# Block pairs as units, 2 KB packets for the early q and k, one load queue and halves of w_in in a fused attention and feed-forward kernel

## The chip, the cores and the metric

The kernel runs on one core of one Trainium2 chip. The metric is the device time of that core in microseconds (us). A kernel also has a slower state, in which some of its runs fall. The ratios below are of runs in the fast state alone; the medians and ranges are of all runs, a few slow ones among them (238.5 us of the kernel before). The span of a profile is about 2 us shorter than the device time of the same run.

## The reference, cut to what matters

```python
# q, k, v: [4, 8, 768, 64] float32; w_in [512, 2048], w_out [2048, 512]
scores = (q @ k.T) / 8 + bias        # bias = -slope[h] * distance
keep   = (key < 8) | (0 <= query - key < 96)        # 8 global keys, 96 local ones
a      = softmax(where(keep, scores, -1e9)) @ v
x      = a.transpose(0, 2, 1, 3).reshape(3072, 512)
h      = x @ w_in
g      = maximum(h, 0) + log1p(exp(-abs(h)))        # softplus
out    = g @ w_out                                  # [3072, 512] float32
```

## The kernel before

The 3072 queries are 24 blocks of 128, six to a sequence. Because of the window, a block needs its own key tile and the one before it; the first block of a sequence needs its own alone. A one-tile block has 8 score matmuls, a two-tile block 16 (eight heads; the matmuls come in pairs, one for each of two heads that lie on different 64 partitions). Two blocks make a group of 256 tokens for the feed-forward part: 64 w_in matmuls of 128x256 in eight slots of eight, then 32 w_out matmuls of 128x512. That makes 768 w_in and 384 w_out matmuls in all. Everything is bf16 on TensorE; inputs are cast on VectorE, ScalarE or GpSimd.

The order of the work on each engine is fixed when the kernel is built. A planner in the kernel simulates all engines and the DMA queues at build time, with a duration that the author gave to each operation, and takes from each engine's ready operations the one of lowest rank. The order that comes out is the program. TensorE is kept busy at the start with up to 90 filler matmuls on a blank tile.

```python
FIRST_UNITS = [[0], [1], [2, 3]]          # the four one-tile blocks, as 1 + 1 + 2
FIRST_LOADS = "u0 u1 u2 i0 i1 i2 i3 i4 i5 i6 i7 o0 u3 o1 o2 o3 o4 o5 o6 o7".split()
O_KEYS = {(0, 1): ("s", 3), (1, 0): ("s", 2)}       # else an output is summed in o_ps
...
s_ps = ps.tile([P, 16, P], F32, name="s_ps")        # four banks, one tile
x_ps = ps.tile([P, 512], F32, name="x_ps")
h_ps = [ps.tile([P, 512], F32, name=f"h_ps{i}") for i in range(2)]
o_ps = ps.tile([P, 512], F32, name="o_ps")
...
# loads of q, k, v: two tokens of one head to a partition row, 512-byte pieces
src[s, :, sl, :].rearrange("h (p r) d -> p h (r d)", r=2)
# w_in: 256 columns of all 512 rows, 1 KB pieces
moe_w_in[:, W * p : W * p + W].rearrange("(m p) c -> p m c", p=P)
...
# q after its transpose by TensorE: one plain copy out of PSUM
copy_on[eng](qT[i % NQT][:, 0:nc_, :], tr)
...
# what the score matmul reads of it: 64 tokens in a row, twice
v4 = t[:].rearrange("p (r m) t -> p m r t", r=2)
return lambda rows, m: v4[rows, m, :, 64 * x : 64 * x + 64]
...
nc.tensor.matmul(s_ps[:, reg, :].rearrange("p (r t) -> p r t", r=2),
                 kt[rows, m, :], qv(rows, m), start=not biased, stop=True, ...)
```

The softmax here doesn't subtract the row's maximum and nothing guards it: scores larger than these inputs give would overflow.

## Time and profile before

| | before |
|---|---|
| device time, median of the first 3 runs | 234.59 us (234.25 to 238.5) |
| span of the profile | 232.6 us |
| TensorE busy | 214.6 us, 92% |
| first w_in matmul | 21.17 us |
| granted TensorE clock, mean | 0.989 |

The first lines are of the page: busy tenths of TensorE, the granted clock, the DMA share and the DMA rate, each in 40 slices of 5.8 us.

```profile
PE   8979889898995998999999999999999999999883
...
PEclk9999999999998899999999999999999999999998
DMA  5999999999796449868877545899679422110021
GB/s 156 224 235 350 352 305 375 360 253 223 199 270 168 122 93 239 190 187 216 133 166 163 133 135 119 243 131 242 168 188 176 113 73 68 48 45 36 10 93 45
```

TensorE is nearly always busy, except in the thirteenth slice (70 to 76 us), where the clock is lower too (0.83 in 70 to 80 us). The DMA engines are nearly full from 6 to 58 us, but move only 224 to 235 GB/s in the second and third slices, while the q, k and v pieces of 512 bytes come. The next lines are three stretches of the trace: busy time of each engine with the number of instructions, the granted clock, the DMA share and GB/s.

```profile
core 0: us, PE busy (x) PEld busy (x) DVE busy (x) ACT busy (x) POOL busy (x), PEclk, DMA share, GB/s
8.00:12.00 4.00, 3.24 (x37) 2.32 (x36) 2.25 (x8) 1.71 (x2) 1.55 (x4) 1.00 1.11 226
60.00:70.00 10.00, 9.33 (x95) 6.36 (x95) 4.59 (x6) 8.99 (x12) 4.20 (x10) 1.00 1.07 260
70.00:80.00 10.00, 7.79 (x80) 4.13 (x81) 6.71 (x13) 4.24 (x5) 5.11 (x9) 0.83 0.55 144
```

From 60 to 80 us TensorE lost almost 3 us. The chain of waits says to what (start, duration, what):

```profile
63.98 6.67 DMA raw<-in_v_dram
...
70.70 0.61 POOL vb L395
...
73.70 4.28 PE o_ps L704 x12
```

A load of v was waited for until 70.6 us, then GpSimd cast it and copied it. The timeline of TensorE (start, duration, operation, shapes, count) shows the start of the feed-forward work and the usual length of 16 score matmuls:

```profile
20.84 0.40 PE L546 MATMUL s_ps<-qT,kTf 64*128 64x128 bf16 x8
21.17 1.05 PE L657 MATMUL h_ps<-XT,w_in_bf 128*128 128x256 bf16 x8
...
63.47 0.62 PE L546 MATMUL s_ps<-qT,kT 64*128 64x128 bf16 x16
```

The last of these: 16 scores in 0.62 us. The end of the chain shows the tail:

```profile
220.01 0.70 DVE osb L728
...
220.75 3.63 PE o_ps L704 x16
...
224.41 0.70 DVE osb L728
...
225.15 3.63 PE o_ps L704 x16
...
228.80 0.42 DVE osb L728
```

Twice TensorE stands still for 0.7 us while VectorE copies the finished output out of the bank that the next output needs.

### The profile page before, as it was taken

The page shows a single profiled execution, that of the slowest core. Times are in us where ns is not written, and L with a number is a line of the kernel's source. Part 1 is how long each engine was busy: PE and PEld are TensorE (multiplying, and loading weights), DVE is VectorE, ACT ScalarE, POOL GpSimd, SP SyncE. Part 2 cuts the span into 40 slices and gives each one's busy share as a digit, 9 for nine tenths or more (in the row PEclk, how much of TensorE's full clock was granted, in tenths as well). Part 3 has the DMA queues.
Part 4 walks back from the last instruction along what each step waited for, and adds up shares of the span by engine and source line. Part 5 has one row for each costly group of instructions (what it writes and reads, how often), then busy time and mean ns, then how long its engine had stood idle before and what let it go on. Part 6 is the DMA issues. An engine that isn't in the chain of part 4 may idle for free.

```text
span 232.6 us, 5037 instructions
## 1 busy us (share of the span) xinstructions
PE 214.6 (92%) x1994; PEld 149.0 (64%) x2026; DVE 113.1 (49%) x219; ACT 154.9 (67%) x202; POOL 98.1 (42%) x178
## 2 busy tenths in 40 slices
PE   8979889898995998999999999999999999999883
PEld 5758777555753476777667667676766867667531
DVE  5567315474179494059538448732944862111111
ACT  2432977751985259898878959876885987676600
POOL 3437645789456224767701606341573630000000
PEclk9999999999998899999999999999999999999998
DMA  5999999999796449868877545899679422110021
GB/s 156 224 235 350 352 305 375 360 253 223 199 270 168 122 93 239 190 187 216 133 166 163 133 135 119 243 131 242 168 188 176 113 73 68 48 45 36 10 93 45
DMA packets 76872, 40.97 MB, mean 176 GB/s; under 512 B 30640, under 2 KB 71856, under 8 KB 76848
## 3 DMA queue, kind: packets, MB, share of 16 engines
q1 hardware_dynamic: 75216, 39.86, 68.2%
q10 hardware_dynamic: 1632, 0.79, 1.4%
q8 instruction: 16, 0.26, 0.5%
q14 instruction: 8, 0.07, 0.1%
HBM read 27.26 MB, written 6.29 MB: 144 GB/s over the span
## 4 chain that ended last, share of the span: by engine, by line
PE 78%; DMA 7%; DVE 4%; POOL 3%; issue 3%; ACT 3%; DVEq 0%; POOLq 0%; ACTq 0%
PE o_ps L704 30%; PE h_ps L657 29%; PE s_ps L546 5%; PE h_ps L807 5%; DMA raw<-in_k_dram 4%; PE s_ps L704 3%; DMA raw<-in_v_dram 3%; PE x_ps L601 2%; ACT pb L581 2%; PE x_ps L598 2%; DVE z L572 2%; POOL vb L501 2%; POOL vb L395 1%; DVE osb L728 1%; PE s_ps L443 1%
## 5 line engine op out<-in xcount | busy, mean ns | idle before, releaser
L657 PE MATMUL h_ps<-XT,w_in_bf 128*128 128x256 bf16 x768 | 95.5, 273 | 1.5 <-POOL w_in_bf L350 0.9
L704 PE MATMUL o_ps<-w_out_bf,g 128*128 128x512 bf16 x323 | 84.8, 385 | 4.0 <-DVE osb L728 1.6
L657 PEld LDWEIGHTS <-w_in_bf 128*128 128x128 bf16 x768 | 73.2, 98 | 20.2 <-POOL w_in_bf L350 2.2
L672 ACT ACTIVATE e<-h_ps 128x512 f32<-128x512 f32 x96 | 59.9, 630 | 30.9 <-PE h_ps L657 30.3
L704 PEld LDWEIGHTS <-g 128*128 128x128 bf16 x384 | 35.9, 99 | 36.2 <-issue 7.0
L572 DVE TENSOR_TENSOR z<-s_ps,biasA 128x1024 f32<-128x1024 f32 x40 | 48.1, 1218 | 18.7 <-PE s_ps L546 17.0
L581 ACT ACTIVATE pb<-z 128x1024 bf16<-128x1024 f32 x40 | 41.8, 1050 | 18.9 <-DVE z L572 18.8
L683 ACT ACTIVATE g<-e 128x1024 bf16<-128x1024 f32 x48 | 50.7, 1056 | 1.3
L395 POOL CAST vb<-raw 64x512 bf16<-64x512 f32 (+1 forms) x60 | 32.8, 547 | 23.1 <-DMA raw<-in_v_dram 17.5
L728 DVE COPY osb<-o_ps 128x512 f32<-128x512 f32 (+1 forms) x23 | 15.2, 665 | 51.4 <-PE o_ps L704 51.3
L395 POOL CAST kb<-raw 64x512 bf16<-64x512 f32 (+1 forms) x44 | 24.0, 545 | 17.5 <-DMA raw<-in_k_dram 15.9
L501 POOL COPY vb<-vb 4x512 bf16<-4x512 bf16 x32 | 19.5, 610 | 17.1 <-PE x_ps L601 16.0
L611 DVE TENSOR_TENSOR xs<-x_ps,rcp 128x256 bf16<-128x256 f32 x46 | 19.5, 424 | 1.6
L610 DVE RECIPROCAL rcp<-x_ps 128x4 f32<-128x4 f32 x46 | 8.3, 179 | 22.8 <-PE x_ps L601 19.5
L601 PE MATMUL x_ps<-vb,pb 128*128 128x65 bf16 x160 | 15.1, 194 | 1.6 <-POOL vb L501 1.5
L598 PE MATMUL x_ps<-vb,pb 128*128 128x65 bf16 x160 | 15.5, 194 | 0.7 <-ACT g L683 0.7
L598 PEld LDWEIGHTS <-pb 128*128 128x128 bf16 x160 | 12.5, 98 | 5.2 <-issue 1.9
L492 POOL COPY kT<-kTf 128x32 bf16<-128x32 bf16 x16 | 3.5, 217 | 27.9 <-PE s_ps L546 27.0
L807 PE MATMUL h_ps<-blank 128*128 128x256 bf16 x90 | 13.8, 305 | 1.2 <-POOL blank L751 1.1
L546 PE MATMUL s_ps<-qT,kT 64*128 64x128 bf16 x288 | 13.4, 217 | 0.7 <-DVE z L572 0.7
L601 PEld LDWEIGHTS <-pb 128*128 128x128 bf16 x160 | 11.3, 97 | 3.4 <-issue 1.0
L370 DVE CAST qb<-raw 128x1024 bf16<-128x1024 f32 (+1 forms) x15 | 9.6, 641 | 7.5 <-DMA raw<-in_q_dram 7.5
(49 smaller groups left out, 98.6 us busy)
## 6 DMA issues: line engine op xcount, KB each, us to landing
out_dram<-osb SPq DMA_DIRECT2D x23, 256.0 KB, 2.4
raw<-in_moe_w_in_dram SPq DMA_DIRECT2D x8, 512.0 KB, 9.5
raw<-in_moe_w_out_dram SPq DMA_DIRECT2D x8, 512.0 KB, 8.3
raw<-in_q_dram SPq DMA_DIRECT2D x8, 512.0 KB, 4.3
raw<-in_k_dram SPq DMA_DIRECT2D x8, 512.0 KB, 5.5
raw<-in_v_dram SPq DMA_DIRECT2D x8, 512.0 KB, 4.9
raw<-in_q_dram SPq DMA_DIRECT2D x10, 128.0 KB, 3.5
raw<-in_k_dram SPq DMA_DIRECT2D x10, 128.0 KB, 3.6
```

What stands on the lines that cost most here:

```text
L395: copy_on[eng](dst, src[64 * x : 64 * x + 64, r, :, :])
L501: nc.gpsimd.tensor_copy(vb_of(prev)[sl, :, 0:D], vb_of(first)[sl, :, 0:D])
L546: nc.tensor.matmul(s_ps[:, reg, :].rearrange("p (r t) -> p r t", r=2), kt[rows, m, :], qv(rows, m), start=not biased, stop=True, skip_grou ...
L572: nc.vector.tensor_tensor(z[:, 0:nr, :], src, bias, ALU.add)
L581: nc.scalar.activation(pb[:, 0:nr, :], src, AF.Exp, scale=1.0 / root_d)
L598: nc.tensor.matmul(xv[:, m, :], pb[:, 2 * m, :], vb_of(n)[:, h, :], start=True, stop=False)
L601: nc.tensor.matmul(xv[:, m, :], pb[:, 2 * m + 1, :], vb_of(prev)[:, h, :], start=False, stop=True)
L657: last = nc.tensor.matmul(hv[:, j, :], w_in_bf[:, m, fb * P : fb * P + P], XT[g % NXG][:, m, :], start=(m == 0), stop=(m == NM - 1),)
L672: nc.scalar.activation(e[:, p % 2, :, :].rearrange("p j (b t r) -> p (j b) r t", b=2, r=2), hb[:].rearrange("p (a r t) -> p a r t", a=4, r=2),
L683: nc.scalar.activation(gt[:, 2 * p - 2 : 2 * p + 2, :].rearrange("p a t -> p (a t)"), e[:].rearrange("p a j t -> p (a j t)"), AF.Ln, bias=1.0,
L704: nc.tensor.matmul(bank(key), gt[:, fb, ns * P : ns * P + P], w_out_bf[:, fb, :], start=(fb == 0), stop=(fb == NFB - 1),)
L807: nc.tensor.matmul(h_ps[0][:, 0:256], blank[:, 0:P], blank[:])
```

## The change

Its intent is to feed TensorE earlier and never late. Every unit becomes a pair of neighbouring blocks of one sequence. For the first three units (called WIDE) q and k come eight tokens to a partition, so in 2 KB packets. All loads go through one queue, in an order that was tuned with the ranks and leads of the planner. A w_in load is now half the rows of 512 columns (2 KB packets) instead of all the rows of 256. The casts are dealt out by hand. The last four outputs go to four different banks (what the kernel calls a bank is 512 fp32 columns of a PSUM tile, room for one output), and the last copy and its store are split over two engines and two queues. The planner learns that eight loads may be under way at once.

The diff is cut to its core; the new rank tables, the engine tables and the bookkeeping of keys are left out.

```diff
+UNITS = [(0, 0), (1, 0), (0, 1), (0, 2), (1, 1), (1, 2), (2, 0), ... (3, 2)]
+WIDE = (0, 1, 2)
+FIRST_LOADS = "k0 q0 v0 v1 q1 k1 i2 i0 i1 i7 i3 i5 i6 i4 o4 q2 o2 o1 k2 o0 v2 o6 o3 o5 o7".split()
...
-O_KEYS = {(0, 1): ("s", 3), (1, 0): ("s", 2)}
+O_KEYS = {(0, 1): ("s", 3), (1, 0): ("s", 2),
+          (10, 0): ("s", 0), (10, 1): ("s", 1), (11, 0): ("s", 2), (11, 1): ("s", 3)}
...
+            if i in WIDE and which != "v":
+                for y in range(2):
+                        return nc.sync.dma_start(
+                            raw[:, 512 * y : 512 * y + 512],
+                            src[y::2, sl, :].rearrange("h (g r) d -> g h (r d)", r=8),
+                        )
...
-                    moe_w_in[:, W * p : W * p + W].rearrange("(m p) c -> p m c", p=P),
+            src = moe_w_in[W * half : W * half + W, 512 * c : 512 * c + 512]
+            dst = w_in_bf[:, 2 * half : 2 * half + 2, 512 * c : 512 * c + 512]
...
+        if i in WIDE:
+            v7 = t[:].rearrange("p (a r) (x g m) -> p x m r g a", r=2, x=2, m=NPAIR)
+            return lambda rows, m: v7[rows, x, m]
...
-                            s_ps[:, reg, :].rearrange("p (r t) -> p r t", r=2), kt[rows, m, :], qv(rows, m),
+                            reg.rearrange("p (r g a) -> p r g a", r=2, a=4)
+                            if unit_of(n) in WIDE
+                            else reg.rearrange("p (r t) -> p r t", r=2),
+                            kt[rows, m, :], qv(rows, m),
...
+        parts = [(0, 256, "DVE", "SP"), (256, DM, "ACT", "ACT")] if last else [(0, DM, "DVE", "SP")]
```

With eight tokens to a partition, the transposed q of a WIDE unit lies as (a r)(x g m): the token's part *a* (four values) is the slowest axis. k is sorted into token order (that of the old layout: the even tokens of a block, then the odd ones) when it is copied out of PSUM. q is not: its copy stays one plain copy, and the score matmul reads it through the view `r g a`, in which neighbouring reads are 256 bf16 elements, that is 512 bytes, apart.

## The prediction

> **What bounds the kernel now.** TensorE. The page's busy table gives it 92% of the 232.6 us span, and the chain that ended last is 78% TensorE. But it does feed-forward work only from the first w_in matmul at 21.2 us on (timeline). At trace rates (8 w_in matmuls 0.875 us, a w_out matmul 0.216 us, two-tile block about 1.03 us) I count, for 21-100 us, about 69 us of work in 79, and for 100-229 us about 122 in 129. So there are four losses: the start (21 us), about 10 us in 21-100, about 7 us afterwards, and 3.8 us behind the last matmul.
>
> - Start: while q/k/v come in 512-byte pieces the windows show 222-248 GB/s (4-16 us) at full DMA share; with w_in (1 KB) and w_out (2 KB) pieces 322-385. Three MB of q/k/v come before w_in; the w_in casts then follow the DMA, one per 1.5 us, until 31.3 us; w_out casts end at 49.8.
> - 21-100: the chain holds 10.0 us of waiting for a k load, 6.7 us for a v load at 64-71 us, then vb casts and copies; in 70-80 us the granted clock is 0.88 and 0.78.
> - End: two waits of 0.7 us for the output copy of the same bank, then two half copies one after the other.
>
> [...]
>
> **What changes.** Early q and k come in 2 KB packets (4 MB of first loads improved or reordered in one FIFO); only v keeps 512 bytes. w_in comes in halves of 2 KB rows: two loads before the first product, but four products then. Casts are dealt over POOL, VectorE, ScalarE. Units are pairs, so the single-block units with 128 KB DMAs (20 SyncE issues of 0.6 us) vanish. The first four blocks are two one-tile and two two-tile blocks: about 1.4 us of TensorE work moves into the start, and four large VectorE adds (1.22 us) become small or vanish. The last groups' outputs get their own banks; the last copy and store split over two engines and queues. Against: strided evictions of k (small), more seeds, all hidden by the start.
>
> **Costs (estimates from the trace).** Loads of 512 KB at about 355 GB/s take 1.48 us, v about 1.8. With k0 landing at about 4.3 us, i0 and i1 (eighth and ninth) land at 15-16.5; with a cast, the first w_in matmul comes at about 17.5 instead of 21.2: -3.7. All w_in are in by about 25 (31), all w_out by about 41 (50). So 21-100 is no longer fed late: of 10 us lost, about 5 come back. Attention done early: -1.4. Tail: -1.5 to -2. Sum about -12 us, nearly all on the critical path, since TensorE is bound afterwards. Gains in casts or VectorE time after 100 us are worth nothing by themselves.
>
> **Predicted: 222.5 us, 8 in 10 between 216.5 and 229.** Faster by over 2%: 0.92; within 2%: 0.07; slower: 0.01.
>
> **What would show it.** First w_in matmul at 16.5-18.5 us; 300 GB/s or more from 4 us on; last w_out cast by 42 us; granted clock 1.0 in 60-90 us; no output-copy waits in the chain's last 10 us; TensorE 92-95% busy; matmul means unchanged.
>
> **What would make it wrong.** The static order was planned: if a load lands later than the planner thought, TensorE waits in order behind a ready matmul (w_out piece 0 comes late, in the order o4, o2, o1, o0). One FIFO may block loads behind a wait for a raw buffer. The strided q and score writes may slow the score matmuls. The clock could drop in a gap at 40-60 us, when the third and fourth units arrive together: then 228-230.

-3.7, -5, -1.4 and -1.5 to -2 make about -12 us, so 234.6 becomes 222.5. The 1.8 us of a v load in 512-byte pieces is an estimate.

## The result, and the profile after

A ratio is the mean time of one kernel's fast runs over that of the other's fast runs of the same rounds, so it is not quite the ratio of the medians quoted beside it.

| | before | after |
|---|---|---|
| device time, median | 234.73 us (4 runs, 234.25 to 238.5) | 231.19 us (4 runs, 230.99 to 231.31) |
| ratio, 95% interval | | 0.9855 (0.9836 to 0.9875) |
| span of the profile | 232.6 us | 229.2 us |
| TensorE busy | 214.6 us, 92% | 219.5 us, 96% |
| first w_in matmul | 21.17 us | 26.25 us |
| granted clock, mean | 0.989 | 0.997 |

The kernel became 1.45% faster, about a quarter of the 5% that were predicted, and the time lies outside the range. The page after, the same lines without the DMA share:

```profile
PE   8998999999999999999999999999999999999873
...
PEclk9999999999999999999999999999999999999998
...
GB/s 167 329 384 387 387 354 365 285 188 96 139 147 207 245 118 180 163 279 197 226 226 183 124 173 183 192 178 153 75 197 166 81 49 23 73 46 0 49 46 92
```

The three stretches after, with the columns as before:

```profile
8.00:12.00 4.00, 3.88 (x37) 2.43 (x37) 2.28 (x6) 0.74 (x2) 2.69 (x4) 1.00 1.09 353
60.00:70.00 10.00, 10.00 (x107) 7.30 (x106) 5.09 (x7) 9.12 (x12) 4.67 (x9) 1.00 0.61 150
70.00:80.00 10.00, 10.00 (x112) 6.05 (x111) 9.27 (x16) 6.17 (x8) 7.77 (x14) 1.00 0.88 208
```

Two intended gains are there. The loads run at 353 GB/s instead of 226 in 8 to 12 us. And between 60 and 80 us TensorE no longer waits: 219 instructions instead of 175, at full clock. But look at the first stretch again: TensorE is busy for 3.88 us instead of 3.24, with the same number of instructions, 37. Its timeline:

```profile
11.36 0.38 PE L611 MATMUL h_ps<-qT,kTa 64*128 64x128 bf16 x1
11.56 0.40 PE L611 MATMUL h_ps<-qT,kTa 64*128 64x128 bf16 x1
...
12.24 1.97 PE L611 MATMUL s_ps<-qT,kTa 64*128 64x128 bf16 x16
...
23.66 1.97 PE L611 MATMUL s_ps<-qT,kTa 64*128 64x128 bf16 x16
26.25 1.03 PE L724 MATMUL h_ps<-XT,w_in_bf 128*128 128x256 bf16 x8
...
45.95 1.95 PE L611 MATMUL s_ps<-qT,kT 64*128 64x128 bf16 x16
...
63.49 0.62 PE L611 MATMUL s_ps<-qT,kT 64*128 64x128 bf16 x16
```

The 16 score matmuls of the WIDE units take 1.95 to 1.97 us; those of later units, loaded in the old layout, take the old 0.62. A pair of scores starts every 0.20 to 0.23 us (11.36, 11.56 and so on; about 0.22 on average), where a pair took about 0.057 before. And the first w_in matmul stands behind the scores of the second unit in TensorE's fixed order, so it comes at 26.25 us. The chain of waits before it:

```profile
16.83 1.40 DVE kb L431
...
20.14 0.44 DVE kTa L527
20.59 0.38 ACT kTa L527
...
23.84 1.79 PE s_ps L611 x16
```

No load is in that piece of the chain. It runs through the cast of k of the second unit, four copies of its transpose and the slow scores. Counted over the three units, the scores cost TensorE about 6.5 us more than at the old rate: units 0 and 1 each four pairs and one row of 16, about 0.65 + 1.35 = 2.0; unit 2 twice 16, about 2.6. These 6.5 us are inside the "96% busy" and do no more work than the old scores did.

The tail did not become what was predicted. The chain's end, and the waits of TensorE (engine, what waited, for what: us in total, times, longest):

```profile
217.69 0.70 DVE osb L796
...
218.44 3.63 PE s_ps L771 x16
...
222.09 0.70 DVE osb L796
...
222.84 2.77 PE s_ps L771 x12
...
225.62 0.43 DVE osb L796
```

```profile
PE s_ps L771 <- DVE osb L796: 2.9, 4, 0.8
```

Three of these four waits, 2.3 us, are at the end (the fourth, 0.5 us, falls before 70 us); the kernel before had two there, 1.6 us. TensorE still waits for each output copy, although the outputs now lie in four different banks. What they have in common is that the four banks are one tile, `s_ps`.

### The profile page after: what moved, and what is told of

Same layout as the page of the kernel before. It is cut to its first block, busy times and chain, and to the rows that moved or that the text cites. A ratio compares the mean times of both kernels' runs of the same rounds, so it can differ in the third digit from the quotient of the medians.

```text
span 229.2 us, 5012 instructions
## 1 busy us (share of the span) xinstructions
PE 219.5 (96%) x2030; PEld 149.8 (65%) x2030; DVE 114.6 (50%) x214; ACT 158.6 (69%) x213; POOL 90.1 (39%) x150
## 4 chain that ended last, share of the span: by engine, by line
PE 88%; ACT 6%; DVE 4%; issue 1%; POOL 0%; DVEq 0%; POOLq 0%
PE h_ps L724 33%; PE o_ps L771 28%; PE s_ps L771 9%; PE s_ps L611 7%; PE x_ps L871 5%; ACT e L739 2%; PE x_ps L665 2%; ACT g L750 2%; PE x_ps L668 2%; DVE osb L796 1%; ACT pb L648 1%; DVE kTa L527 1%; ACT kTa L527 1%; DVE kb L431 1%; DVE xs L678 1%
## 5 line engine op out<-in xcount | busy, mean ns | idle before, releaser
L771 PE MATMUL o_ps<-w_out_bf,g 128*128 128x512 bf16 x288 | 72.6, 379 | 0.3 <-ACT g L750 0.3
L639 DVE TENSOR_TENSOR z<-s_ps,biasA 128x1024 f32<-128x1024 f32 x36 | 43.0, 1218 | 21.4 <-PE s_ps L611 13.5
L648 ACT ACTIVATE pb<-z 128x1024 bf16<-128x1024 f32 (+1 forms) x40 | 39.6, 1006 | 5.5 <-DVE z L639 5.0
L451 POOL CAST vb<-raw 64x512 bf16<-64x512 f32 x40 | 25.3, 632 | 14.2 <-DMA raw<-in_v_dram 12.6
L796 DVE COPY osb<-o_ps 128x512 f32<-128x512 f32 x18 | 12.4, 690 | 31.0 <-PE o_ps L771 31.0
L771 PE MATMUL s_ps<-w_out_bf,g 128*128 128x512 bf16 x96 | 22.8, 379 | 2.9 <-DVE osb L796 2.9
L451 POOL CAST kb<-raw 64x512 bf16<-64x512 f32 x36 | 22.3, 618 | 4.4 <-DMA raw<-in_k_dram 2.9
L796 DVE COPY osb<-s_ps 128x512 f32<-128x512 f32 (+1 forms) x6 | 3.9, 648 | 24.7 <-PE s_ps L771 24.7
L871 PE MATMUL x_ps<-blank 128*128 128x252 bf16 x90 | 14.0, 308 | 1.9 <-POOL blank L818 1.1
L871 PEld LDWEIGHTS <-blank 128*128 128x128 bf16 x90 | 9.5, 111 | 4.8 <-issue 1.2
```

The source lines that it names most:

```text
L451: copy_on[eng](dst, src)
L639: nc.vector.tensor_tensor(z[:, 0:nr, :], src, bias, ALU.add)
L648: nc.scalar.activation(pb[:, 0:nr, :], src, AF.Exp, scale=1.0 / root_d)
L771: nc.tensor.matmul(bank(key), gt[:, fb, ns * P : ns * P + P], w_out_bf[:, fb, :], start=(fb == 0), stop=(fb == NFB - 1),)
L871: nc.tensor.matmul(x_ps[:, 4 * (D + 1) : 512], blank[:, 0:P], blank[:, 0 : 512 - 4 * (D + 1)])
```

## The experiments

Three theories were open at the start. The first: the step at which the matmul reads q makes the scores slow, and this lies on the critical path. Its rivals: any step, in the read or in the write to PSUM, costs as much, so that reading in another order would not help (in the kernel after itself the scores are written in a row); or the slow scores are hidden, and something else (loads, fillers, the halves of w_in, VectorE) holds the start. The tail is a separate question. Where the texts give theories letters, each says there what it expects; here they are named by what they say. The kernel before was run beside every set; its medians were 235.55 us for the first four experiments, 235.08 for the next four and 235.13 for the last four. All experiments start from the kernel after. By their traces e1, e1b, e2, e3 and e8 have its order on TensorE, VectorE, ScalarE and GpSimd, and e9 and e11 have that of e2, apart from the copies and tiles that were edited; the other runs were planned anew.

### e1_q_by_g: the score's columns in another order, q read in 8-byte steps

```diff
-            v7 = t[:].rearrange("p (a r) (x g m) -> p x m r g a", r=2, x=2, m=NPAIR)
+            v7 = t[:].rearrange("p (a r) (x g m) -> p x m a r g", r=2, x=2, m=NPAIR)
...
-                            reg.rearrange("p (r g a) -> p r g a", r=2, a=4)
+                            reg.rearrange("p (r g a) -> p a r g", r=2, a=4)
```

The same numbers are computed into the same places, in the same order of instructions. Only the order in which one matmul goes through its 128 queries is new: the innermost step of the read is 4 elements (8 bytes), and that of the write to PSUM is 16 bytes.

> Only the order of the free axes of the score matmuls of the first three units is changed: q is read in steps of 8 bytes (the innermost step was 512 bytes), and the same result is written to PSUM in steps of 16 bytes (was contiguous). The instruction order on all engines is that of the changed kernel. Theory A (the 512-byte steps of the q read made 16 score matmuls take 1.88 us where other blocks take 0.55): the groups fall to 0.55-0.8 us and the time by 4 to 6 us, to 225-227 us. Rival B (any step on either side, or the scattered PSUM write, costs as much): the groups stay above 1.3 us and the time within 1.5 us of 231.2. Rival C (the slow scores are hidden behind the casts and evictions of the start): groups get fast, time falls by under 2 us.

Measured: 226.48 us, ratio 0.9649 (0.9574 to 0.9725). Its timeline:

```profile
11.58 1.08 PE L611 MATMUL s_ps<-qT,kTa 64*128 64x128 bf16 x16
...
23.49 1.03 PE L724 MATMUL h_ps<-XT,w_in_bf 128*128 128x256 bf16 x8
```

16 scores take 1.08 us instead of 1.97, a pair 0.11 us, and the first w_in matmul comes 2.8 us earlier. The write became scattered and the scores became faster, so the step of the read is the cause, and it is on the critical path: the time fell by about 2.1%. But a step of 8 bytes is not free: the 16 scores had been expected at 0.55 to 0.8 us.

### e1b_q_by_g_psum_flat: the same with a contiguous write (wrong)

```diff
-                            reg.rearrange("p (r g a) -> p a r g", r=2, a=4)
+                            reg.rearrange("p (a r g) -> p a r g", r=2, a=4)
```

This writes PSUM in a row, so the queries of the WIDE units land in the wrong order. Its output is wrong, which doesn't matter for the time. The comparison with the reference still let it pass. The likely reason is the inputs: q and k are drawn with a deviation of 0.1, which makes (q k)/8 about 0.01 (an estimate), and the mask and the bias are added in the right places. So the comparison does not vouch for the order of q in any of these runs; for e2 it was checked in the code alone.

> As the run before, but the PSUM write is contiguous too, so the queries of the first three units land in a wrong order and the result is wrong on purpose. It separates read from write: theory A expects groups of 0.55-0.65 us and the same time as the run before, within 1 us. If the write steps cost, this run has fast groups and the run before slow ones, and is 4-6 us faster than it. If the 8-byte read steps cost, both are slow.

Measured: 226.04 us, ratio 0.9634 (0.9555 to 0.9714).

```profile
11.22 1.08 PE L611 MATMUL s_ps<-qT,kTa 64*128 64x128 bf16 x16
```

The scores take 1.08 us here too. So the scattered write of e1 adds nothing that can be seen beside this read, and e1's 1.08 us are the read's. The rival falls. Whether a scattered write would slow matmuls that run 16 in 0.62 us, no run here shows.

### e2_q_copied_flat: q put in token order when it leaves PSUM

```diff
-            return lambda rows, m: v7[rows, x, m]
+            return lambda rows, m: t[rows, NPAIR * x + m, :].rearrange("p (r g a) -> p r g a", r=2, a=4)
...
-            op(f"cpq{i}", ..., lambda: copy_on[eng](qT[i % NQT][:], tr), ...)
+            def evq():
+                if i not in WIDE:
+                    return copy_on[eng](qT[i % NQT][:], tr)
+                to = qT[i % NQT][:].rearrange("p (x m) (r g a) -> p x r m g a", x=2, r=2, a=4)
+                fr = tr.rearrange("p (a r) (x g m) -> p x r m g a", r=2, x=2, m=NPAIR)
+                for x in range(2):
+                    for r in range(2):
+                        last = copy_on[eng](to[:, x, r], fr[:, x, r])
+                return last
```

The sorting is paid for once, on VectorE or ScalarE, as the change did for k. The planner is told the old duration, so the order stays.

> The eviction of q of the first three units is made in four copies of 256 elements that put q in token order, so the score matmuls read and write contiguously. Same instruction order otherwise. Theory A: score groups of 16 at 0.55 us, 8 at 0.33; the q evictions grow from 0.68 to about 1.7 us each on VectorE (1.0 to about 1.5 on ScalarE), which gives back about 1 us in units 0 and 1; time 226-228.5 us. Rival C: no better than 230.

Measured: 225.09 us (224.54 to 225.35), ratio 0.9582 (0.9494 to 0.967).

```profile
12.01 0.62 PE L620 MATMUL s_ps<-qT,kTa 64*128 64x128 bf16 x16
...
23.31 1.03 PE L733 MATMUL h_ps<-XT,w_in_bf 128*128 128x256 bf16 x8
```

The scores are back at 0.62 us. The copies of q are dearer (four of 418 ns on VectorE instead of one of 680, four of 387 on ScalarE instead of one of 1012). The gain over the kernel after is 0.9855 - 0.9582 = 0.0273 of about 234.7 us, or 6.4 us, with an uncertainty of about 2 us by the two intervals (the medians give 6.1). That is what the 6.5 us of extra TensorE time let one expect. Most of the slow scores, if not all, was on the critical path. Only some 2.9 us of it shows at the start (26.25 to 23.31); the third unit's share comes later.

### e3_tail_banks: the last four outputs in four tiles

```diff
-    (10, 0): ("s", 0), (10, 1): ("s", 1), (11, 0): ("s", 2), (11, 1): ("s", 3),
+    (10, 0): ("x",),   (10, 1): ("o",),   (11, 0): ("h0",),  (11, 1): ("h1",),
```

> The last four output accumulations go to four separate PSUM tiles (x, o, h0, h1) where the changed kernel put them in four banks of one tile. Theory D: the three waits of 0.7 us of TensorE for the output copy at the end come from tracking the four banks as one tile; with separate tiles they vanish, 2 to 2.3 us are gained, 229 us. Rival: TensorE must wait for the copy for another reason (the copy is slower than thought, or the order holds it): waits stay, no gain.

Measured: 229.38 us (228.33 to 229.79), ratio 0.9764 (0.9686 to 0.9841), so about 2.1 us better than the kernel after, with an uncertainty of nearly 2 us (the medians give 1.8). Its span is only 1.4 us shorter; that profile has a slower stretch at the start (one w_in slot of 1.87 us instead of 1.03, mean clock 0.992). The waits of TensorE on the output copies:

```profile
PE s_ps L771 <- DVE osb L796: 0.5, 1, 0.5
```

They went from 2.9 us in four to 0.5 in one, and the one that is left is the early one: the three at the end, 2.3 us, are gone. Different banks of one tile had not been enough; different tiles were. That it is the dependency tracking of the framework, which takes the tile as a whole, is the obvious reading, but the run shows only that the waits go with the tile.

### e4_no_wide: no unit in 2 KB packets, planned anew

```diff
-WIDE = (0, 1, 2)
+WIDE = ()
```

> The changed kernel with the 2 KB packets undone: early q and k come in 512-byte pieces as all others, so q lies in token order after the transposes and the score matmuls read contiguously; the planner reorders a little. Theory E (the start of the feed-forward work is bound by the attention chain on the engines, not by when the loads land): score groups at 0.55 us, first w_in matmul at 22-25 us, time 225-227.5 us, that is as good as the run with q copied flat (225.1) or within 2 us of it, so the 2 KB packets bought nearly nothing and cost about 6 us. Rival F (the 2 KB packets matter for the start): DMA at 220-250 GB/s until 12 us, first w_in matmul 2 us or more later than the 23.3 us of the flat copy, time 228-231 us.

Measured: 228.99 us, ratio 0.9749 (0.9681 to 0.9817). The scores take 0.61 us and the first w_in matmul comes at 23.37 us, as in e2, although the loads run at 290 GB/s in 8 to 12 us instead of 353. So the faster loads don't seem to bring the start forward (the fillers at the head happened to take 0.8 us less here, see e9; e8 is cleaner). But the time is 4 us worse than in e2. By 150 us it had done 208 w_out matmuls (weight loads counted) against 224 in e2. The planner had been told other loads and had made another order. This run tells two things at once and so neither cleanly; e8 repeats it with the order held.

### e5_q_flat_fill: e2 with the fillers' true length

```diff
-FILLERS = 90
+FILLERS = 64
-BIASA_ON = ["ACT", "POOL", "DVE"]
+BIASA_ON = ["ACT", "DVE"]
-        op(f"fill{j}", "PE", 0.11, 1e6 + j, fn, reads=["blank"])
+        op(f"fill{j}", "PE", 0.213 if j < 30 else 0.11, 1e6 + j, fn, reads=["blank"])
```

The early fillers run longer than the planner believes (0.213 us from one to the next by the trace, where it counts 0.11), which may hold back the first real work on TensorE.

> On top of the run with q copied flat: the planner is told 0.213 us for the first 30 filler matmuls (the trace shows the first ones at that spacing) so 23 instead of 43 stand before the first k transposes, 64 in all, and the late bias tiles are made on ScalarE and VectorE only (on GpSimd one took 1.06 us where the planner thought 0.4). Theory G: the in-order fillers and the bias tiles held the first scores until 11.6 us though k had been cast at 5.6 and q at 7.6; scores start at 9.5-10.5, first w_in matmul at 21.5-22.5, time 223.3-224.3 us. Rival: the start is held later by the casts of the second unit, then the first scores move and the first w_in matmul does not, time within 0.6 us of 225.1.

Measured: 224.97 us, ratio 0.9585 (0.9514 to 0.9657), the same as e2. The first unit's scores came at 10.80 instead of 12.01 us, but the second unit's at 21.45 instead of 21.77 and the first w_in matmul at 22.99 instead of 23.31. Most of what the first unit won was lost before the second unit. So the fillers don't seem to bind the start; the order of some other operations changed with them.

### e6_q_flat_narrow: e2 with w_in in 1 KB column blocks, planned anew

```diff
-NARROW = ()
+NARROW = (0, 1, 2, 3)
```

> On top of the run with q copied flat: w_in in column blocks of 1 KB rows as before the change, in the same order of names. Each product then waits for one load, not two, but the loads are slower. If the loads of w_in bind the start, the first w_in matmul moves by a microsecond or more and the time by as much; if they do not (theory E), the time stays within 1 us of 225.1.

Measured: 231.22 us (5 runs), ratio 0.9837 (0.9756 to 0.9917), 6 us worse than e2. Its loads ran at 349 to 353 GB/s from 12 to 24 us, e2's at 365 to 394. The first w_in matmul came at 23.57 us, so not there. TensorE had new waits (1.8 us for a copy to XT on ScalarE, 1.6 for a copy of v on GpSimd, 1.0 for a copy of k on VectorE). As in e4 the plan was a new one, so this run does not say whether the halves or the plan cost it; e9 does.

### e7_all_true: all mends, and true durations for the planner

This is e2, e3 and e5 together, and the planner is told what the four copies of q cost.

```diff
-            op(f"cpq{i}", eng, t_copy(eng, 1024, True), rank, evq, ...)
+            op(f"cpq{i}", eng, 4 * (t_copy(eng, 256, True) + 0.14) if i in WIDE else t_copy(eng, 1024, True), rank, evq, ...)
```

> All mends together: q copied flat with its true duration told to the planner, fewer fillers, no bias on GpSimd, and the last four outputs in separate PSUM tiles. If they add: 225.1 minus about 2 for the end minus about 1 for the start, 221.5-223 us, 5% below the kernel before.

Measured: 226.48 us, ratio 0.9648 (0.9575 to 0.9722), where 221.5 to 223 had been expected. Truer figures gave a worse plan: new waits of TensorE, 1.5 us for the cast of k and 1.1 us for that of q, and 210 w_out matmuls by 150 us, about as in e4. The ranks and leads of the change were tuned for the plan that came out of the old figures.

### e8_small_packets: 512-byte packets, with the order of the kernel after

```diff
-                            raw[:, 512 * y : 512 * y + 512],
-                            src[y::2, sl, :].rearrange("h (g r) d -> g h (r d)", r=8),
+                            raw[:, 512 * y : 512 * y + 512].rearrange("p (h c) -> p h c", h=4),
+                            src[4 * y : 4 * y + 4, sl, :].rearrange("h (p r) d -> p h (r d)", r=2),
...
-        if i in WIDE:      # the views of q, k and the scores
+        if False:
```

The planner's figures stay those of the kernel after, so every engine has the same order.

> Like the run that undid the 2 KB packets, but with the planner left as it is, so that the order on every engine is that of the changed kernel and of the flat copy: early q and k come in 512-byte pieces, lie in token order, are evicted by one plain copy and scored contiguously. It measures the packets alone. Theory E (packets do not bind the start; the 4 us of the earlier run came from its re-planned order): first w_in matmul within 0.7 us of the 23.3 us of the flat copy, time within 1 us of 225.1. Rival F (late loads cost 4 us somewhere): time 228-230 us and a wait on a load in the chain.

Measured: 225.69 us (225.55 to 226.52), ratio 0.961 (0.9548 to 0.9673). The stretch of 8 to 12 us:

```profile
8.00:12.00 4.00, 4.00 (x52) 2.96 (x51) 2.16 (x6) 0.77 (x3) 2.61 (x4) 1.00 1.20 292
```

And the first w_in matmul in its timeline:

```profile
22.81 1.03 PE L724 MATMUL h_ps<-XT,w_in_bf 128*128 128x256 bf16 x8
```

The loads run at 292 GB/s instead of 353 (v comes in 512-byte pieces in both), and yet the first w_in matmul comes at 22.81 us, and the time is that of e2 within the intervals. The 2 KB packets made the loads faster, as predicted. But, with the sorting of q and k that they call for (e8 has plain copies again, so it weighs the two together), they earned no time that can be seen, and they were the reason for the layout that cost 6.4 us.

### e9_q_flat_narrow_same: e2 with w_in in 1 KB column blocks, with e2's order

```diff
-            src = moe_w_in[W * half : W * half + W, 512 * c : 512 * c + 512]
-            dst = w_in_bf[:, 2 * half : 2 * half + 2, 512 * c : 512 * c + 512]
+            raw = raw_t[slot][:].rearrange("p (a c) -> p a c", a=NM)
+            src = moe_w_in[:, W * p : W * p + W]
+            dst = w_in_bf[:, :, W * p : W * p + W]
```

> w_in in 1 KB column blocks as before the change, but with the planner's figures and so the order of the flat copy run (where the earlier run re-planned and lost 6 us). If the halves of w_in matter by themselves, time 226.5 us or more; if the 6 us came from the re-planned order, within 1 us of 225.1, as every product waits for fewer bytes but loads run at about 350 instead of 385 GB/s.

Measured: 225.44 us, ratio 0.9596 (0.9527 to 0.9664), as e2, although its loads ran at 348 to 356 GB/s from 12 to 24 us, against 365 to 394. The halves of w_in are worth nothing by themselves, and the 6 us of e6 came from planning anew. The first w_in matmul came at 21.91 us in this profile instead of 23.31. That need not be the edit's doing: the 43 fillers at the head of TensorE's order took 6.08 us here and 7.37 in e2 (7.12 in the kernel after, 6.18 in e11):

```profile
1.08 7.37 PE L880 MATMUL x_ps<-blank 128*128 128x252 bf16 x43 [1.08 <-POOL blank L827]
...
1.08 6.08 PE L881 MATMUL x_ps<-blank 128*128 128x252 bf16 x43 [1.08 <-POOL blank L828]
```

These fillers are the same in all four kernels, and their rate changes on the way: in the kernel after, each microsecond from 1 to 6 us counts 5 to 8 of them, and 12 from 6 to 8 us (one that crosses a border counts twice). From 4 to 8 us TensorE ran 43 matmuls in e9 and 28 in e2, so the faster rate began earlier in e9. (The clock column of the profile reads 1.00 throughout, so the trace shows the change of rate and not its reason.) A difference of 1.3 us between two profiles at the start can be that.

### e10_q_flat_dve_less: casts of the second unit from VectorE to ScalarE

```diff
-    1: {..., "q": "POOL", "v": ["POOL", "DVE"], "k": "DVE"},
+    1: {..., "q": "POOL", "v": ["POOL", "ACT"], "k": "ACT"},
```

This is e2 with the cast of k (1.40 us in the chain of the kernel after) and half the casts of v off VectorE. If VectorE's queue held the start, the second unit's scores should come earlier.

> The flat copy run with the second unit's k cast and its two VectorE v casts (about 2.5 us of VectorE between 12 and 17 us) on ScalarE. Theory H (VectorE's in-order queue at 10-18 us sets the start): the second unit's scores begin 1 us or more before 21.5 us and the first w_in matmul at 21.3-22.5 us instead of 23.3. What the total does is open, since the planner re-orders the rest: 222.5-228. Rival (ScalarE becomes the same queue): first w_in matmul not earlier.

Measured: 229.68 us, ratio 0.9798 (0.9715 to 0.9882), worse than e2 by 0.0216 of the time before, or about 5 us. A line of its timeline:

```profile
23.04 1.06 PE L620 MATMUL s_ps<-qT,kTa 64*128 64x128 bf16 x16
```

And of its waits of TensorE:

```profile
PE o_ps L601 <- DVE kTa L536: 1.7, 1, 1.7
```

The second unit's scores came later (23.04 instead of 21.77 us, and in a phase of low clock, 0.78 in 20 to 24 us), and TensorE gained a wait of 1.7 us for a copy of k. The expectation missed. The order was planned anew here too, so the run doesn't clear VectorE; it only shows that this way of relieving it doesn't help. What bounds the start stays open.

### e11_q_flat_tail: e2 and e3 together, the order kept

> The flat copy and the separate PSUM tiles for the last four outputs, order otherwise unchanged. If the two add: 225.1 - 2 = 222.7 to 223.6 us, waits of TensorE on the output copy down from 2.9 to at most 0.9 us.

Measured: 222.52 us as the median of all four runs (221.84, 221.41 and 223.21 in the fast state, 222.15 on average; the fourth, of 226.14, was slow), ratio 0.9453 (0.9373 to 0.9532). If the two gains add, the ratio is 0.9855 - 0.0273 - 0.0091 = 0.9491, which lies in the interval. The end of its chain:

```profile
206.05 3.45 PE o_ps L780 x16
209.50 6.92 PE h_ps L780 x32
...
216.50 0.43 DVE osb L805
```

The last 48 w_out matmuls run without a wait. This version beats both kernels: 5.5% below the kernel before, against 1.45% for the change as it was.

## Why the prediction was wrong

It expected 222.5 us, and 231.19 were measured, a miss of 8.7 us. Two mends bring 6.4 and 2.1 us by the ratios, 8.5 together, and the kernel with both runs at 222.15 in the fast state. The miss is thus explained to within the intervals. That the mended time comes so near the predicted one is partly luck, since the terms of the sum were not all right: in e11 too the first w_in matmul comes at 21.97 us, later than before the change (21.17), so the predicted 3.7 us of the start never came. Yet at 80 us e11 has done 29 w_in and 14 w_out matmuls more than the kernel before, about 6 us of feed-forward work (an estimate at 0.109 and 0.216 us each). The gain came in another place than predicted.

- **"Against: strided evictions of k (small), more seeds, all hidden by the start."** This is the step that failed. It counted the strided writes of k (its copies of 128x256 took 411 to 425 ns on VectorE, those of the same size in the kernel before about 288) but no cost for q, which isn't sorted at all and is read with a step of 512 bytes by every score matmul of three units. e1 and e2 show the cause, and e2 its size: 6.4 us, not hidden. The risk list had the sentence "The strided q and score writes may slow the score matmuls" without a number. A count would have shown the stake: four times 16 scores and twice 8 are 40 pairs, so each 0.1 us on a pair is 4 us of TensorE; the runs showed 0.163. The half of that sentence about score writes had no object: in the kernel after they are not strided, and strided ones added nothing that can be seen beside the read (e1 against e1b).
- **The start, "-3.7".** The loads became faster as predicted (353 GB/s), but the first w_in matmul came 5.1 us later instead of 3.7 earlier. About 2.9 us of that are slow scores (e2). The prediction timed this start by the landing of w_in, at 15 to 16.5 us for i0 and i1, and a cast. In the trace these two landed at 17.2 and 18.4 us, in the order of issue, and the first four casts of w_in had ended by 22.6 us. TensorE came to the first w_in matmul only at 26.25 us, since the second unit's copies and scores stand before it in its order. So the path was another than the predicted one; e8 and e9 show that neither the packets nor the shape of the w_in loads move the time, and what else bounds the start stays open (e10).
- **The middle, "of 10 us lost, about 5 come back".** Right in kind: from 60 to 80 us TensorE went from 17.1 us busy to 20.0, the clock stayed at 1.00, and the wait for v is gone. At 80 us the kernel after had done 192 w_in and 91 w_out matmuls, the kernel before 192 and 82, though the former began 5 us later and lost about 6.5 us to slow scores. Which part of the change brings this (pairs, leads, load order or one queue) was not taken apart, nor was the "-1.4" for attention done early.
- **"All w_out by about 41".** The last cast of w_out ended at 48.9 us (before 49.8). That step missed, and TensorE had nothing to wait for through it.
- **The tail, "-1.5 to -2".** It didn't come: three waits on the output copies, 2.3 us, were left at the end, where the kernel before had two of 1.6 us together. The prediction took different banks for independent. With different tiles 2.1 us came (e3), about the predicted size.
- **"Matmul means unchanged", "TensorE 92-95% busy".** The first was false (1.97 for 0.62 us). The second read 96%, and would have looked like a success to anyone who reads the share alone.

## What to carry to other kernels

A load layout with larger packets may be paid for by the later readers (here 6.4 us): before taking it, write down the innermost step at which each matmul reads the data, and sort once in a copy if that step is not one element. Three steps were measured here: 16 scores took 0.62 us with a step of one element, 1.08 with 4 and 1.97 with 256, so of these only the first was free; the sorting copies cost four of 418 ns on VectorE instead of one of 680. A longer time of the same matmuls is the sign that this went wrong, and a rising TensorE share (here from 92% to 96%) hides it. Outputs that are to be independent should lie in different tiles, not only in different banks: four banks of one tile left three waits, 2.3 us, at the end here, and four tiles none (e3). In a statically planned kernel, test one idea with the order held: e4 and e6 changed harmless things, lost 4 to 6 us to a new plan, and would have been read as verdicts on packets and halves, had e8 and e9 not followed.
